# Weights split two tiles at a time, in operations twice as wide

## The chip, the cores and the metric

The kernel runs on one core of a Trainium2 chip. TensorE multiplies matrices into PSUM; VectorE, ScalarE and GpSimd work on elements; SyncE issues the transfers between HBM and SBUF. Each engine works through its own list of instructions in order and waits on semaphores for the others. The metric is device time in microseconds of one execution, as the median of several runs; one further execution was profiled.

## The reference

Two stages follow each other. The first is gated linear attention with 4 batches, 8 heads, 768 positions and head dimension 48:

```python
f = 1.0 / (1.0 + np.exp(-f_logit))
for t in range(S):
    state = f[:, :, t, :, None] * state + np.einsum('bhd,bhe->bhde', k[:, :, t], v[:, :, t])
    y[:, :, t] = np.einsum('bhd,bhde->bhe', q[:, :, t], state)
```

The second takes its output as x (4 x 768 x 384) through a gated network with a convolution of three positions along the sequence:

```python
h = np.maximum(x @ w_in, 0.0)                       # 384 -> 1024
conv_out[s] = sum_k conv_w[k] * h[s + k - 1]
out = (h * 1.0 / (1.0 + np.exp(-conv_out))) @ w_out  # 1024 -> 384
```

The three weights w_in (384 x 1024), conv_w (3 x 1024) and w_out (1024 x 384) come in as float64, all else as float32.

## The kernel before

**Recurrence.** The sequence of each batch is cut into 6 chunks of 128 positions, 24 chunks in all, numbered n. A chunk goes through these steps: the gate (exp and ln of f_logit on ScalarE, L183 and L184, loaded into fb in groups of three chunks); a running sum over positions by a product with a triangle of ones (pl, L209), from which fi and fd are made by exp (L213, L214); k times fi and q times fd (L226, L227; from the third chunk on, q on GpSimd); transposes of both (ptk, ptq, then kT, qT); the scores pa (L291), masked into am on VectorE (L293); the state (pk, L305, and stmp, st); and the values py (L328, L331), which are written as high and low part into xT (L339, L340).

**Network.** For every half sequence u, mm1 multiplies xT with w_in in eight slices f (ph, L368), ScalarE takes the relu (hb, L371), ScalarE and VectorE do the convolution (L373, L379, L380), ScalarE a tanh (L382) and VectorE the gating (L383). mm2 splits the result into gh and gl (L398, L399), multiplies them with w_out (po, L405), and ScalarE copies the output out (ob, L408). ph and po share two PSUM buffers with the tag mm.

**Weight split.** TensorE is used here with float32r operands, so each weight is wanted as a high part (what float32r holds) and a low part (the remainder). The function split_f64 makes both from the two 32-bit words of a float64: ScalarE takes the absolute value of the upper word (L101), VectorE clamps it (L102), changes the exponent's bits (L103), ScalarE clears the sign again (L104), VectorE puts the sign back (L105) and takes out the exponent (L106), and ScalarE writes the high part (L111). The low part of w_in and of the first four tiles of w_out is summed on TensorE from three products in a buffer pz (L120 to L122), from low (L118), and copied back by VectorE (w_in) or ScalarE (w_out) at L123. For the last four tiles of w_out it is made on VectorE (L113 to L115). A tile is 128 rows of a weight by 512 columns (w_in, 3 x 2 tiles) or 384 columns (w_out, 8 tiles): 14 tiles, and one small call for conv_w (24 x 128).

**Scratch.** The working pair ms (m and s side by side) lies in a buffer of the tag gl, low in one of the tag ob, the raw conv_w in one of gh. gl and gh are later the operands of mm2, ob its output; each tag has two buffers.

**What sets the order.** Every piece of work gets a number (plan, from L423 on), in units of chunks, and the pieces are emitted in the order of these numbers: the loads of w_in at -2.3 and -1.1, its splits from -0.7 and 0.9 in steps of 0.1, conv_w at 1.3, the loads of w_out at 1.3 and 1.0, its splits from 2.1 in steps of 0.35. From this the framework's scheduler, by its own modelled durations and the waits between the pieces, lays down the order of each engine's instructions before anything runs. From chunk 8 on, the recurrence's visits to TensorE (scores, state, values) are tied to one another by hand.

## Time and profile before

| | us |
|---|---|
| median of three runs | 376.55 |
| the three runs | 374.24, 376.55, 377.16 |
| the profiled execution | 371.6 |
| its span | 369.9 |

The profile's span runs from the first to the last recorded instruction; 1.7 us of the profiled execution lie around it. The granted TensorE clock was 0.987 of full speed over the span. Engines are called PE (TensorE's matmuls), PEld (its weight loads), DVE (VectorE), ACT (ScalarE), POOL (GpSimd) and SP (SyncE, which issues the transfers). A row of a group of instructions reads: line, engine, operation, written tile <- read tiles, shape, count | busy time and mean duration in ns | idle time of the engine just before them and what ended most of it. A row of one tile's instructions gives minimum, median and maximum duration in ns, and the first and the last start in us. A row of the timeline reads: start, duration, engine, line, operation, and in brackets how long the engine had been idle and for whom. A row of the waits reads: who <- for whom: us in all, times, the longest.

### The profile page before, as it was taken

What the parts mean: (1) busy time and instruction counts of PE and PEld (TensorE: products, weight loads), DVE (VectorE), ACT (ScalarE), POOL (GpSimd) and SP (SyncE); (2) the same over time, 40 slices, a digit from 0 to 9 for tenths busy, and PEclk for the clock granted to TensorE, in tenths of its full rate; (3) what the DMA queues carried; (4) which work ended last, traced back from release to release, by engine and by line L of the source; (5) the groups of instructions that cost most, each with busy time, mean ns of one, the idle gap of its engine ahead of it and who ended that gap; (6) DMA issues with size and microseconds to landing.
All of it is one profiled execution on the core that took longest, in us unless ns stands there. A gap on an engine that the chain in (4) does not pass through costs nothing.

```text
span 369.9 us, 7330 instructions
## 1 busy us (share of the span) xinstructions
PE 346.4 (94%) x2775; PEld 315.4 (85%) x2775; DVE 290.4 (79%) x455; ACT 237.9 (64%) x428; POOL 53.0 (14%) x72
## 2 busy tenths in 40 slices
PE   4799899989799998999999999999999999999993
PEld 1566678778699997999899999999999999999993
DVE  4799999999899877888689897689868875575620
ACT  3779777897977667567856566457464545665530
POOL 1111222112111410240101421041010000000000
PEclk9699999999999999999999999999999999999998
DMA  7999344315312450335113331341011002101011
GB/s 228 394 356 365 98 139 123 99 37 161 81 29 88 101 171 20 96 88 165 51 44 90 88 114 50 74 110 51 24 43 35 23 0 56 43 2 43 23 43 51
DMA packets 28853, 36.04 MB, mean 97 GB/s; under 512 B 10847, under 2 KB 20106, under 8 KB 28810
## 3 DMA queue, kind: packets, MB, share of 16 engines
q1 hardware_dynamic: 28810, 35.49, 32.1%
q8 instruction: 24, 0.39, 0.5%
q14 instruction: 19, 0.16, 0.1%
HBM read 28.37 MB, written 4.75 MB: 90 GB/s over the span
## 4 chain that ended last, share of the span: by engine, by line
PE 59%; ACT 14%; DVE 14%; DMA 6%; issue 4%; SPq 1%; ACTq 0%; DVEq 0%
PE po L405 23%; PE ph L368 20%; PE py L331 4%; DMA fb<-in_f_logit_dram 4%; PE pa L291 4%; PE py L328 3%; DMA wis<-in_moe_w_in_dram 2%; DVE g L379 2%; ACT fb L183 2%; DVE am L293 1%; PE ptk L249 1%; PE ptq L249 1%; PE pk L305 1%; ACT hb L371 1%; ACT g L373 1%
## 5 line engine op out<-in xcount | busy, mean ns | idle before, releaser
L368 PE MATMUL ph<-xT,wi 128*128 128x384 f32 x576 | 112.2, 344 | 4.5 <-ACT ob L408 2.5
L368 PEld LDWEIGHTS ph<-xT,wi 128*128 128x128 f32 x576 | 100.6, 188 | 8.2 <-ACT ob L408 3.7
L405 PE MATMUL po<-wo,gh 128*128 128x384 f32 x384 | 99.7, 340 | 0.2 <-ACT hb L371 0.2
L405 PEld LDWEIGHTS po<-wo,gh 128*128 128x128 f32 x384 | 69.6, 188 | 0.7 <-ACT hb L371 0.5
L405 PE MATMUL po<-wo,gl 128*128 128x384 f32 x192 | 66.0, 344 | 0.0
L379 DVE SCALAR_TENSOR_TENSOR g<-hb,cw,g 128x384 f32<-128x384 f32 (+1 forms) x64 | 43.5, 682 | 13.1 <-ACT g L373 12.5
L382 ACT ACTIVATE g<-g 128x768 f32<-128x768 f32 (+1 forms) x32 | 27.1, 848 | 38.7 <-DVE g L380 38.5
L371 ACT ACTIVATE hb<-ph 128x384 f32<-128x384 f32 x64 | 31.2, 489 | 23.5 <-PE ph L368 23.2
L380 DVE SCALAR_TENSOR_TENSOR g<-hb,cw,g 128x384 f32<-128x384 f32 (+1 forms) x64 | 41.8, 653 | 2.9
L399 DVE TENSOR_TENSOR gl<-g,gh 128x1024 fp32r<-128x1024 f32 (+4 forms) x34 | 32.2, 957 | 14.7 <-ACT gh L398 14.6
L383 DVE SCALAR_TENSOR_TENSOR g<-g,hb 128x768 f32<-128x768 f32 (+1 forms) x32 | 30.6, 957 | 14.1 <-ACT g L382 14.0
L227 POOL TENSOR_TENSOR qp<-qp,fd 128x384 f32<-128x384 f32 x22 | 28.9, 1313 | 87.7 <-ACT fd L214 72.1
L373 ACT ACTIVATE g<-hb,cw 128x384 f32<-128x384 f32 (+1 forms) x64 | 39.3, 619 | 2.2 <-ACT hb L371 0.4
L398 ACT CAST gh<-g 128x1024 fp32r<-128x1024 f32 (+4 forms) x34 | 26.5, 802 | 20.8 <-PE po L405 18.4
L405 PEld LDWEIGHTS po<-wo,gl 128*128 128x128 f32 x192 | 36.1, 188 | 1.1 <-issue 0.2
L293 DVE COPY_PREDICATED am<-mask,pa 128x1024 f32<-128x1024 uint8 x24 | 31.6, 1315 | 0.3
L291 PE MATMUL pa<-qT,kT 48*128 48x128 f32 x384 | 28.8, 286 | 0.4 <-ACT qT L251 0.4
L331 PE MATMUL py<-am,v 128*48 128x128 f32 x384 | 26.8, 277 | 1.6 <-DVE am L293 1.6
L226 DVE TENSOR_TENSOR kp<-kp,fi 128x384 f32<-128x384 f32 x22 | 22.7, 1033 | 6.8 <-ACT fi L213 6.6
L291 PEld LDWEIGHTS pa<-qT,kT 48*128 48x128 f32 x384 | 23.9, 187 | 3.8 <-issue 1.7
L331 PEld LDWEIGHTS py<-am,v 128*48 128x48 f32 x384 | 20.1, 122 | 6.8 <-DVE am L293 2.3
L328 PE MATMUL py<-qT,st 128*112 128x128 f32 x168 | 22.9, 275 | 0.1
(107 smaller groups left out, 432.1 us busy)
## 6 DMA issues: line engine op xcount, KB each, us to landing
kp<-in_k_dram SPq DMA_DIRECT2D x24, 256.0 KB
qp<-in_q_dram SPq DMA_DIRECT2D x24, 256.0 KB
fb<-in_f_logit_dram SPq DMA_DIRECT2D x24, 192.0 KB
v<-in_v_dram SPq DMA_DIRECT2D x24, 192.0 KB
out_dram<-ob SPq DMA_DIRECT2D x24, 192.0 KB
wis<-in_moe_w_in_dram SPq DMA_DIRECT2D x6, 512.0 KB
wos<-in_moe_w_out_dram SPq DMA_DIRECT2D x8, 384.0 KB
xT<-xT SPq DMA_DIRECT2D x48, 48.0 KB
```

The source lines that it names most:

```text
L291: nc.tensor.matmul(pa[:, j, p, :], kT[r, p, :], qT[r, p, :], start=True, stop=True)
L293: ready.setdefault(n, []).append(nc.vector.copy_predicated(am, mask, pa).ins)
L328: nc.tensor.matmul(py[:HP + D, p, :], s_b[n % 2][:, p, :], qT[:, p, :], start=(p == 0), stop=False)
L331: nc.tensor.matmul(py[HP * j:HP * j + D, p, :], vt[:, 2 * p + j, :], am[:, j, p, :], start=not inter and p == 0, stop=(p == NP - 1))
L368: nc.tensor.matmul(ph, wi[:, t, wl, f * P:(f + 1) * P], xts[b, hf][:, t, xl, :], start=(i == 0), stop=(i == 3 * KT - 1))
L371: nc.scalar.activation(hb[:, 2:HS + 2], ph, AF.Relu, scale=0.5)
L373: nc.scalar.activation(cv, hb[:, 1:n + 1], AF.Copy, scale=cw[:, 1, f:f + 1])
L379: nc.vector.scalar_tensor_tensor(cv, hb[:, 2:n + 2], cw[:, 2, f:f + 1], cv, ALU.mult, ALU.add)
L380: nc.vector.scalar_tensor_tensor(cv, hb[:, 0:n], cw[:, 0, f:f + 1], cv, ALU.mult, ALU.add)
L383: nc.vector.scalar_tensor_tensor(cv, cv, 1.0, h_b[:, fp:fp + 2, 1:n + 1], ALU.add, ALU.mult)
L399: nc.vector.tensor_tensor(lo, g[:, f:f + k], hi.bitcast(F32), ALU.subtract)
L405: nc.tensor.matmul(po, g[:, f, :], wo[:, f, wl, :], start=(i == 0), stop=(i == 3 * NF - 1))
```

## The change

split_f64 now takes several tiles at once: raw, hi and lo have a dimension k of tiles, and every operation on VectorE and ScalarE runs over all of them, 1024 or 768 elements in place of 512 or 384. Only the products on TensorE and the copy back of the low part run tile by tile; both accumulators pz of a pair are open together.

A new entry of the table CFG, kin=[[(0, 1), (1, 2)], [(0, 2), (2, 1)]], groups the three tiles of each half of w_in: tile 0 alone and tiles 1 and 2 as a pair in the first half, tiles 0 and 1 as a pair and tile 2 alone in the second. w_out goes in four pairs, emitted where the first tile of each stood. The scratch m lies in a buffer of gl, and s and low each in one of gh, all three of 1024 elements; the raw conv_w moves from gh to ob.

```diff
-    def split_f64(raw, n, hi, lo, nm, tile=0):
+    def split_f64(raw, hi, lo, nm, tile=0):
-        pr = raw.rearrange("p (n w) -> p n w", w=2)
-        lw, hw = pr[:, :, 0], pr[:, :, 1]
-        r = raw.shape[0]
-        ms = wk.tile([P, 2, WC], I32, tag="gl", name=f"ms{nm}")
-        m, s = ms[:r, 0, :n], ms[:r, 1, :n]
+        pr = raw.rearrange("p k (n w) -> p k n w", w=2)
+        lw, hw = pr[:, :, :, 0], pr[:, :, :, 1]
+        r, k, n = hw.shape
+
+        def scratch(tag, t, dt):
+            return wk.tile([P, 2 * WC], dt, tag=tag, name=f"{t}{nm}")[:r, :k * n].rearrange("p (k n) -> p k n", k=k)
+
+        m, s = scratch("gl", "m", I32), scratch("gh", "s", I32)
...
-        low = wk.tile([P, WC], F32R, tag="ob", name=f"low{nm}")[:, :n]
+        low = scratch("gh", "l", F32R)
         nc.vector.scalar_tensor_tensor(low, lw.bitcast(U32), 2.0 ** -52, sf, ALU.mult, ALU.mult)
-        pz = ps.tile([P, WC], F32, tag="mm", name=f"pz{nm}", bufs=2)[:, :n]
-        nc.tensor.matmul(pz, ident, mf, start=True, stop=False)
-        nc.tensor.matmul(pz, negr, hi, start=False, stop=False)
-        nc.tensor.matmul(pz, idr, low, start=False, stop=True)
-        (nc.vector.tensor_copy if CFG["ez"][tile] == "d" else nc.scalar.copy)(lo, pz)
+        for x in range(k):
+            pz = ps.tile([P, WC], F32, tag="mm", name=f"pz{nm}_{x}", bufs=2)[:, :n]
+            nc.tensor.matmul(pz, ident, mf[:, x], start=True, stop=False)
+            nc.tensor.matmul(pz, negr, hi[:, x], start=False, stop=False)
+            nc.tensor.matmul(pz, idr, low[:, x], start=False, stop=True)
+            (nc.vector.tensor_copy if CFG["ez"][tile + x] == "d" else nc.scalar.copy)(lo[:, x], pz)
...
-        raw = wk.tile([nk * NF, 2 * P], I32, tag="gh", name="cws")
+        raw = wk.tile([nk * NF, 2 * P], I32, tag="ob", name="cws")
...
             plan(CFG["wil"][i] + 0.01 * kt, lambda kt=kt, i=i: load_w_in(kt, i))
-            plan(CFG["wis"][i] + 0.1 * kt, lambda kt=kt, i=i: split_w_in(kt, i))
+        for kt, m in CFG["kin"][i]:
+            plan(CFG["wis"][i] + 0.1 * kt, lambda kt=kt, m=m, i=i: split_w_in(kt, m, i))
...
-        plan(CFG["wos"] + f * CFG["wo"], lambda f=f: split_w_out(f))
+        if f % 2 == 0:
+            plan(CFG["wos"] + f * CFG["wo"], lambda f=f: split_w_out(f, 2))
```

The lines of the file move by 3 to 6 (L101 becomes L104, L111 L114, L123 L127, L293 L297, L368 L372, L382 L386, L405 L409). The order of the instructions changes with the pieces. On ScalarE at the start of the program, the first two tiles of w_in stood one after the other ahead of the first chunk's fi and fd (mswi_0_188 and mswi_0_206 are the scratch of tiles 0 and 1):

```order
L101 ACTIVATE mswi_0_188<-wis_119 128x512
L101 ACTIVATE mswi_0_206<-wis_119 128x512
L104 ACTIVATE mswi_0_188<-mswi_0_188 128x512
L213 ACTIVATE fi_130<-pl_127 128x384
L214 ACTIVATE fd_129<-pl_127 128x384
L104 ACTIVATE mswi_0_206<-mswi_0_206 128x512
L111 CAST wi<-mswi_0_188 128x512
L222 COPY ft_all<-pl_127 48x4 x2
```

In the new program the same place reads (mwi_0_188 is tile 0's m, mwi_0_207 that of tiles 1 and 2):

```order
L104 ACTIVATE mwi_0_188<-wis_119 128x512
L107 ACTIVATE mwi_0_188<-mwi_0_188 128x512
L217 ACTIVATE fi_130<-pl_127 128x384
L218 ACTIVATE fd_129<-pl_127 128x384
L104 ACTIVATE mwi_0_207<-wis_119 128x1024
L114 CAST wi<-mwi_0_188 128x512
L226 COPY ft_all<-pl_127 48x4 x2
L255 COPY kT_161<-ptk_156 128x512
```

Tile 1 has left the place ahead of fi and fd and stands behind them, together with tile 2; the cast of tile 0 and the copies follow it.

On VectorE, in the middle of w_out's split, the order before was this (mswo_678, mswo_731 and mswo_783 are three of the last four tiles, g the network's first slices):

```order
L102 TENSOR_SCALAR mswo_731<-mswo_731 128x384
L113 SCALAR_TENSOR_TENSOR mswo_678<-wos_357,mswo_678 128x384
L316 TENSOR_TENSOR st_100<-stmp_1_806,ft_all 48x4x48
L103 TENSOR_SCALAR mswo_731<-mswo_731 128x384
L114 TENSOR_TENSOR mswo_678<-mswo_678,wo 128x384
L115 TENSOR_TENSOR wo<-mswo_678 128x384
L105 SCALAR_TENSOR_TENSOR mswo_731<-wos_357,mswo_731 128x384
L106 TENSOR_SCALAR mswo_731<-mswo_731 128x384
L379 SCALAR_TENSOR_TENSOR g_689<-hb,cw,g_689 128x384
```

In the new program it is this (mwo_645 and mwo_740 are the two pairs of the last four tiles):

```order
L105 TENSOR_SCALAR mwo_645<-mwo_645 128x768
L121 SCALAR_TENSOR_TENSOR lwo_566<-wos_424,swo_558 128x768
L344 TENSOR_TENSOR xT_0_302<-py_532,xT_0_302 112x4x128
L106 TENSOR_SCALAR mwo_645<-mwo_645 128x768
L297 COPY_PREDICATED am_96<-mask_86,pa_578 128x1024
L108 SCALAR_TENSOR_TENSOR mwo_645<-wos_340,mwo_645 128x768
L319 TENSOR_TENSOR stmp_0_597<-pk_588,st_100 48x192
L109 TENSOR_SCALAR swo_646<-mwo_645 128x768
L105 TENSOR_SCALAR mwo_740<-mwo_740 128x768
```

One instruction stands where two stood, and the last two pairs begin a chunk earlier, beside the fourth chunk's mask (am_96) and not beside the network's first slices.

On ScalarE around the first tanh, the order before had exp and ln of the next group (fb_1091) ahead of it:

```order
L183 ACTIVATE fb_1091<-fb_1091 128x1152
L371 ACTIVATE hb<-ph_2_753 128x384
L251 COPY kT_920<-ptk_915 128x512
L184 ACTIVATE fb_1091<-fb_1091 128x1152
L251 COPY qT_927<-ptq_922 128x512
L104 ACTIVATE mswo_783<-mswo_783 128x384
L373 ACTIVATE g_689<-hb,cw 128x384
L213 ACTIVATE fi_932<-pl_929 128x384
L214 ACTIVATE fd_931<-pl_929 128x384
L101 ACTIVATE mswo_851<-wos_357 128x384
L382 ACT_TABLE_LOAD
L382 ACTIVATE g_689<-g_689 128x2x384
```

In the new program that group is fb_1038, and it comes after two tanh and before a third (g_657 is the network's first half sequence):

```order
L386 ACTIVATE g_657<-g_657 128x2x384
L187 ACTIVATE fb_1038<-fb_1038 128x1152
L377 ACTIVATE g_657<-hb,cw 128x384
L188 ACT_TABLE_LOAD
L188 ACTIVATE fb_1038<-fb_1038 128x1152
L255 COPY kT_867<-ptk_862 128x512
L255 COPY qT_874<-ptq_869 128x512
L386 ACT_TABLE_LOAD
L386 ACTIVATE g_657<-g_657 128x2x384
```

Two loads of activation tables have come in there, one ahead of the ln and one ahead of the next tanh.

More of the change, by code (lines that the diff above doesn't have):

```diff
@@ L22 @@
 F_MIN = 2.0 ** -64
-CFG = dict(ez="ddddddaaaavvvv", ng=8, hp=4000, tb=2, groups=[3, 3, 3, 3, 3, 3, 3, 3], sg=3, f1=2.6, g1=2.6, gv=2, gl=5.2, g=3.9, l=3.2, a=1.8, b=0.8, s=0.2, v=0.5, wil=(-2.3, -1.1), wis=(-0.7, 0.9), cw=1.3, wol=(1.3, 1.0), wos=2.1, wo=0.35, m1=0.5, m1s=0.9, m2=1.5, m2s=1.2, ek=(12, 24), ec='d', er='p', tp=0, tf=2, nw=2, gd=0, q0=2, lf=3, kpool=2, eg='d', eq='p', es='d', em='d', ew='p', xb=3, nf=6, fe='a', kb=4, qb=3, vb=4, lv=2.2, cb=1, sb=3, fi=1)
+CFG = dict(ez="ddddddaaaavvvv", ng=8, kin=[[(0, 1), (1, 2)], [(0, 2), (2, 1)]], hp=4000, tb=2, groups=[3, 3, 3, 3, 3, 3, 3, 3], sg=3, f1=2.6, g1=2.6, gv=2, gl=5.2, g=3.9, l=3.2, a=1.8, b=0.8, s=0.2, v=0.5, wil=(-2.3, -1.1), wis=(-0.7, 0.9), cw=1.3, wol=(1.3, 1.0), wos=2.1, wo=0.35, m1=0.5, m1s=0.9, m2=1.5, m2s=1.2, ek=(12, 24), ec='d', er='p', tp=0, tf=2, nw=2, gd=0, q0=2, lf=3, kpool=2, eg='d', eq='p', es='d', em='d', ew='p', xb=3, nf=6, fe='a', kb=4, qb=3, vb=4, lv=2.2, cb=1, sb=3, fi=1)
 @with_exitstack
@@ L116, in split_f64, with raw_in, raw_out @@
             return
-        low = wk.tile([P, WC], F32R, tag="ob", name=f"low{nm}")[:, :n]
+        low = scratch("gh", "l", F32R)
         nc.vector.scalar_tensor_tensor(low, lw.bitcast(U32), 2.0 ** -52, sf, ALU.mult, ALU.mult)
-        pz = ps.tile([P, WC], F32, tag="mm", name=f"pz{nm}", bufs=2)[:, :n]
-        nc.tensor.matmul(pz, ident, mf, start=True, stop=False)
-        nc.tensor.matmul(pz, negr, hi, start=False, stop=False)
-        nc.tensor.matmul(pz, idr, low, start=False, stop=True)
-        (nc.vector.tensor_copy if CFG["ez"][tile] == "d" else nc.scalar.copy)(lo, pz)
+        for x in range(k):
[4 more added lines that the diff above has]
+            (nc.vector.tensor_copy if CFG["ez"][tile + x] == "d" else nc.scalar.copy)(lo[:, x], pz)
     raws = {}
-    def raw_in(kt, i):
-        if kt == 0 and ("i", i) not in raws:
+    def raw_in(i):
+        if ("i", i) not in raws:
             raws["i", i] = wk.tile([P, KT, 2 * WC], I32, tag="g32", name=f"wis{i}")
-        return raws["i", i][:, kt]
-    def raw_out(f):
-        i = f // 4
+        return raws["i", i]
+    def raw_out(i):
         if ("o", i) not in raws:
@@ L136, in raw_out, with split_w_in, split_w_out @@
                             wk.tile([P, 4, 2 * DM], I32, tag="xT", name=f"wos{i}", bufs=CFG["xb"]))
-        return raws["o", i][:, f % 4]
+        return raws["o", i]
     def load_w_in(kt, i):
-        nc.sync.dma_start(raw_in(kt, i), w_in[kt * P:(kt + 1) * P, i * WC:(i + 1) * WC].bitcast(I32))
-    def split_w_in(kt, i):
-        cs = slice(i * WC, (i + 1) * WC)
-        split_f64(raw_in(kt, i), WC, wi[:, kt, 0, cs], wi[:, kt, 1, cs], f"wi{kt}_{i}", KT * i + kt)
+        nc.sync.dma_start(raw_in(i)[:, kt], w_in[kt * P:(kt + 1) * P, i * WC:(i + 1) * WC].bitcast(I32))
+    def split_w_in(kt, k, i):
+        cs, ks = slice(i * WC, (i + 1) * WC), slice(kt, kt + k)
+        split_f64(raw_in(i)[:, ks], wi[:, ks, 0, cs], wi[:, ks, 1, cs], f"wi{kt}_{i}", KT * i + kt)
     def load_w_out(f):
-        nc.sync.dma_start(raw_out(f), w_out[f * P:(f + 1) * P, :].bitcast(I32))
-    def split_w_out(f):
-        split_f64(raw_out(f), DM, wo[:, f, 0, :], wo[:, f, 1, :], f"wo{f}", DFF // WC * KT + f)
+        nc.sync.dma_start(raw_out(f // 4)[:, f % 4], w_out[f * P:(f + 1) * P, :].bitcast(I32))
+    def split_w_out(f, k):
+        split_f64(raw_out(f // 4)[:, f % 4:f % 4 + k], wo[:, f:f + k, 0, :], wo[:, f:f + k, 1, :], f"wo{f}",
+                  DFF // WC * KT + f)
     def load_cw():
         nk = conv_w.shape[0]
-        raw = wk.tile([nk * NF, 2 * P], I32, tag="gh", name="cws")
+        raw = wk.tile([nk * NF, 2 * P], I32, tag="ob", name="cws")
         nc.sync.dma_start(raw, conv_w.bitcast(I32).rearrange("k (f x) -> (k f) x", f=NF))
         c32 = wk.tile([P, WC], F32, tag="ob", name="c32")[:nk * NF, :P]
-        split_f64(raw, P, c32, None, "cw")
+        split_f64(raw.rearrange("p (k x) -> p k x", k=1), c32.rearrange("p (k x) -> p k x", k=1), None, "cw")
         pc = ps.tile([P, nk * NF], F32, tag="mm", name="pc", bufs=2)
```

## The prediction

> **What bounds the kernel now.** I read the page's totals first, then busy time by stretch, then who waits for whom and the timeline around the places that the change touches.
>
> ```profile
> span 369.9 us, 7330 instructions
> PE 346.4 (94%) x2775; PEld 315.4 (85%) x2775; DVE 290.4 (79%) x455; ACT 237.9 (64%) x428; POOL 53.0 (14%) x72
> ```
>
> TensorE is busy in 94% of the span, so all the rest together can give back 23.5 us. Where those lie is read from the stretches (columns: length, busy time of PE, PEld, DVE, ACT and POOL with counts, granted TensorE clock, DMA share, GB/s).
>
> ```profile
> 20.00:40.00 20.00, 19.06 (x218) 13.78 (x217) 19.52 (x41) 17.91 (x42) 3.21 (x3) 1.00 0.89 319
> 40.00:60.00 20.00, 18.85 (x178) 13.95 (x177) 18.99 (x42) 15.32 (x35) 2.97 (x2) 1.00 0.50 128
> 60.00:80.00 20.00, 18.05 (x139) 14.78 (x138) 19.27 (x33) 16.80 (x32) 5.83 (x4) 1.00 0.27 76
> 80.00:103.40 23.40, 20.67 (x180) 17.54 (x179) 21.90 (x37) 21.10 (x35) 3.40 (x4) 1.00 0.39 105
> 103.40:370.00 266.60, 257.18 (x2009) 248.02 (x2006) 198.56 (x282) 156.27 (x268) 34.78 (x43) 0.99 0.23 63
> ```
>
> The weight splits run from 7.5 us to some 90 (rows below), all before the second matrix product (po, L405), which begins at about 103.4, where the last two stretches are cut. In that part the bound is VectorE: 19.5, 19.0, 19.3 of 20 us and 21.9 of 23.4, while TensorE idles 0.94 + 1.15 + 1.95 + 2.73 = 6.8 us. After 103.4 TensorE idles 9.4 us of 266.6 and sets the pace itself. So the change acts on a prefix of 103 us, and whatever lead it has when po begins goes on to the end, since the work behind that point is the same.
>
> **The change part by part.** *Fewer, wider operations.* In w_in two pairs replace four single tiles and two tiles stay single; in w_out four pairs replace eight. Each pair saves one instruction of every kind that was widened. VectorE: 5 kinds (L102, L103, L105, L106, L118) in 2 pairs of w_in and 2 of w_out, 7 kinds (L113 to L115 in L118's place) in the other 2 of w_out: 10 + 10 + 14 = 34 fewer. ScalarE: 3 kinds (L101, L104, L111) in 6 pairs: 18 fewer. The casts and matmuls of the low part stay one per tile. What one saves follows from the durations by width:
>
> ```profile
> L102 DVE TENSOR_SCALAR mswi<-mswi x6: 418/424/428, 7.5 to 28.4; 128x512 f32<-128x512 f32 x6
> L102 DVE TENSOR_SCALAR mswo<-mswo x8: 340/356/1167, 37.0 to 77.9; 128x384 f32<-128x384 f32 x8
> L105 DVE SCALAR_TENSOR_TENSOR mswi<-wis,mswi x6: 675/678/1515, 11.2 to 32.2; 128x512 int32<-128x512 int32 x6
> L105 DVE SCALAR_TENSOR_TENSOR mswo<-wos,mswo x8: 540/555/1111, 40.2 to 83.2; 128x384 int32<-128x384 int32 x8
> L383 DVE SCALAR_TENSOR_TENSOR g<-g,hb 128x768 f32<-128x768 f32 x16 | 15.3, 956 | 8.5 <-ACT g L382 8.5
> L104 ACT ACTIVATE mswi<-mswi 128x512 f32<-128x512 f32 x6 | 3.8, 632 | 0.7 <-DVE mswi L103 0.7
> L398 ACT CAST gh<-g 128x1024 fp32r<-128x1024 f32 x20 | 21.0, 1056 | 11.7 <-PE po L405 11.4
> ```
>
> Two of 384 elements take 2 x 555 = 1110 ns and one of 768 takes 956: 154 ns less. From 384 to 512 a TENSOR_SCALAR grows by 68 ns, so one of 768 is 356 + 3 x 68 = 560 against 712: 152 ns less. On ScalarE 2 x 632 - 1056 = 208 ns less. That is the saving when the next instruction waits for the result. Where it does not, neighbours overlap:
>
> ```profile
> 88.26 0.55 DVE L113 SCALAR_TENSOR_TENSOR mswo<-wos,mswo 128x384 f32<-128x384 uint32 x1
> 88.72 0.56 DVE L114 TENSOR_TENSOR mswo<-mswo,wo 128x384 f32<-128x384 f32 x1
> ...
> 91.75 0.94 DVE L383 SCALAR_TENSOR_TENSOR g<-g,hb 128x768 f32<-128x768 f32 x1
> 92.61 0.55 DVE L226 TENSOR_TENSOR kp<-kp,fi 128x384 f32<-128x384 f32 x1
> 79.75 1.14 ACT L373 ACTIVATE g<-hb,cw 128x384 f32<-128x384 f32 x2
> ```
>
> From start to start 384 elements cost 0.46 us and 768 cost 0.86: only 0.06 saved; of the two ScalarE ones in 1.14 us, each 0.62 long, 0.10 overlaps, so 0.1 is saved there. VectorE therefore gains between 34 x 0.06 = 2.0 and 34 x 0.15 = 5.1 us. In the new order about a third of the wide instructions stand directly behind the one whose result they need, so I take 23 x 0.06 + 11 x 0.15 = 3.0 us, nearer the overlapped end because the engine nearly always has the next one ready. ScalarE's 18 x 0.1 to 18 x 0.2 = 1.8 to 3.6 us I count at nothing: between 20 and 103.4 it idles 2.1 + 4.7 + 3.2 + 2.3 = 12.3 us, which hide it; without that cover they would count whole.
>
> *The first microseconds.* The timeline and the waits at the start:
>
> ```profile
> 7.93 0.43 DVE L103 TENSOR_SCALAR mswi<-mswi 128x512 int32<-128x512 int32 x1
> 9.67 0.66 ACT L101 ACTIVATE mswi<-wis 128x512 f32<-128x512 f32 x1 [2.23 <-DMA wis<-in_moe_w_in_dram]
> ...
> 11.12 0.49 ACT L214 ACTIVATE fd<-pl 128x384 f32<-128x384 f32 x1
> 11.32 1.53 SPq L140 DMA_DIRECT2D wis<-in_moe_w_in_dram  x3
> 12.01 0.62 ACT L111 CAST wi<-mswi 128x512 fp32r<-128x512 f32 x1
> ...
> PE pl L218 <- ACT fd L214: 4.5, 1, 4.5
> SPq L140 <- DMA wis<-in_moe_w_in_dram: 1.3, 1, 1.3
> ```
>
> Before, ScalarE's second L101 (tile 1 of w_in) waits for its transfer until 9.67, and L104 of tile 0, fi and fd stand behind it. Now the first tile goes alone: L103 ends at 8.4, so L104, fi and fd would end near 10.0 where fd ended at 11.6: 1.6 us earlier for TensorE, which idles 4.5 us for fd. Then the first pair waits for tiles 1 and 2. The third transfer landed near 11.3 (the next w_in load, queued for its slot on SP, was let go by it then), and with a wide L101 of 1.06 us and the cast behind it, tile 0's high part is ready at 11.3 + 1.06 + 0.62 = 13.0, where it was at 12.0 + 0.6 = 12.6. Queued behind that wait on ScalarE are the cast, the two copies into ft_all and kT. So it is between -1.6 us and, if those 0.4 and the longer chain of the pair count, +1.0. Going through the rows of VectorE and ScalarE to the second mask copy (am) with the durations above, most of the early lead is gone by then: wide instructions stand ahead of kT, qT and am. I take -0.5.
>
> *Wide instructions ahead of the recurrence.* On an engine that works in order, am (L293, for which TensorE waits) can stand behind 1.0 us where it stood behind 0.55.
>
> ```profile
> PE py L331 <- DVE am L293: 1.6, 3, 0.9
> ```
>
> Six chunks fall in this part. Between 0 and 6 x 0.35 (about half of a wide instruction's length more) = 2.1 us; I take +0.5, as only 3 of 24 visits of py waited at all. Both accumulators of a pair are open at once, in the two PSUM buffers that ph and po use too; the first ph comes behind those, and I put that at 0.
>
> *One more change of activation tables.* The split work gets done sooner, and the scheduler moves the first tanh (L382) ahead of the exp and ln of group 4. In the new order, ln and tanh alternate once more before po: two table loads more on ScalarE.
>
> ```profile
> L382 ACT ACT_TABLE_LOAD x3 | 3.8, 1283 | 0.1
> L184 ACT ACT_TABLE_LOAD x3 | 3.8, 1283 | 0.1
> ...
> 76.09 1.28 ACT L382 ACT_TABLE_LOAD   x1
> 78.66 3.44 PE L368 MATMUL ph<-xT,wi 128*128 128x384 f32 x18 [1.25 <-ACT hb L371]
> 93.88 1.28 ACT L184 ACT_TABLE_LOAD   x1
> 95.18 1.17 ACT L184 ACTIVATE fb<-fb 128x1152 f32<-128x1152 f32 x1
> 96.86 1.28 ACT L382 ACT_TABLE_LOAD   x1
> 101.07 0.44 PE L209 MATMUL pl<-cgh,tri 128*128 128x384 f32 x1 [2.23 <-ACT kT L251]
> ```
>
> 2 x 1.28 = 2.57 us on ScalarE. Both places with loads in this prefix are followed by an idle TensorE, 1.25 and 2.23 us. Between 0 and 2.57; I take their mean, +1.7. [...]
>
> **Sum.** -3.0 + 0 - 0.5 + 0.5 + 1.7 = -1.3 us. The profiled execution took 371.6 us (span 369.9 and 1.7 around it), so it would take 370.3. The median of the three runs is 376.55, 1.3% above the profiled one; on that footing 375.2.
>
> **Rivals.** *The gain comes whole (faster).* If ScalarE hides the extra loads as it idles 5.5 us between 60 and 103.4, and most wide instructions pay the dependent price: VectorE -3.8 to -4.5, ScalarE's shorter chains 0 to -1.5, the start 0 to -1.0, loads 0 to +0.5 spent where they show. That is -3.8 to -6.5, so 370.0 to 372.8. For it: VectorE's 95 to 99%. Against it: TensorE has only 6.8 + 1.6 us to give back, and each load so far reached it.
>
> *ScalarE becomes the bound (slower).* The gate of a later group must land before its exp:
>
> ```profile
> 91.71 1.17 ACT L183 ACTIVATE fb<-fb 128x1152 f32<-128x1152 f32 x1 [1.56 <-DMA fb<-in_f_logit_dram]
> ...
> SPq L241 <- DMA ft<-fd: 17.3, 17, 3.4
> ```
>
> ScalarE waited 1.56 us for group 5's transfer already, and on SP that load now stands behind the decay row's store (L233), and its last chunk behind the decay row's way back (L241), which waits 1.0 us as a rule and 3.4 at worst. Two loads and that delay make 2.57 + 1.0 to 2.57 + 3.4 = 3.6 to 6.0 us on ScalarE, of whose idle 5.5 us in 60 to 103.4 part is fixed by waits. It decides once some 3 us of it come in one piece between tanh and ln: then VectorE's 3.0 us are idle time, and the run is about 4.5 us slower: 381.
>
> [...]
>
> **Chances and range.** The forecast 0.58, the gain whole 0.24, ScalarE the bound 0.13, the port 0.05. About 1%, 3.8 us, is what a measurement of this kernel can tell from no change. So faster by over 1%: 0.24; within 1%: 0.58 + 0.05 = 0.63; slower by over 1%: 0.13. The forecast's own range, from the bounds of its terms that are likely together, is 373 to 378.5; reaching into both rivals, 370.5 to 380 leaves out about 2 in 10.
>
> **What would show it.** Right: 34 fewer instructions on VectorE and 18 fewer operations on ScalarE, the wide ones near 0.95 and 1.17 us; po starting at 100 to 103 us; VectorE still over 93% busy between 20 and 80; four table loads of tanh and four of ln in place of three each; a new TensorE gap of 1 to 2 us near the first tanh. Wrong: po starting before 99 (the gain came whole), or after 105 with ScalarE waiting for fb; TENSOR_SCALARs of 1024 elements far over 0.70 us; or a difference that arises after po has begun, which this reasoning does not have.

## The result, and the profile after

The changed kernel takes 380.67 us (median of 4 runs, 377.42 to 381.28), the kernel before beside it 376.68 (374.24 to 377.16): a ratio of 1.0125, interval 1.0082 to 1.0167. It is 1.2% slower, by more than a measurement of this kernel is uncertain, where 375.2 and no difference were forecast. The profiled execution took 380.79 us.

The totals of the page after, with two rows of its 40 slices (one digit for 9.5 us):

```profile
span 379.1 us, 7259 instructions
PE 352.5 (93%) x2775; PEld 319.4 (84%) x2775; DVE 285.9 (75%) x421; ACT 238.7 (63%) x412; POOL 53.7 (14%) x72
...
PE   5689799996999999899899999999999999999993
...
PEclk9999879998799999999999999999999999999998
```

The counts are as forecast: VectorE 455 to 421, ScalarE 428 to 412 (18 operations fewer, 2 table loads more). VectorE is busy 4.5 us less, and TensorE 6.1 us more for the same 2775 matmuls. What goes with that stands in the last row: the granted clock falls in slices 5 and 6 and again in 10 and 11, where before it fell only in slice 2 and at the end. The stretches, cut where the first second-product matmul (po) begins, at 110.9 (before: 103.4):

```profile
20.00:40.00 20.00, 18.08 (x163) 11.52 (x161) 19.33 (x34) 15.08 (x32) 2.15 (x2) 1.00 0.96 344
40.00:60.00 20.00, 17.68 (x156) 12.91 (x155) 15.92 (x27) 14.45 (x29) 2.19 (x2) 0.83 0.23 57
60.00:80.00 20.00, 20.00 (x168) 17.31 (x166) 19.78 (x29) 17.25 (x30) 6.74 (x3) 1.00 0.46 126
80.00:110.90 30.90, 25.76 (x212) 21.58 (x211) 23.59 (x35) 25.06 (x38) 5.90 (x7) 0.89 0.38 101
110.90:379.00 268.10, 258.60 (x2030) 249.12 (x2026) 197.50 (x281) 157.80 (x271) 34.18 (x43) 0.99 0.23 63
```

Behind po the two kernels take the same, 268.1 and 266.6 us. All is lost ahead of it. Two places stand out: between 40 and 60 us VectorE is busy 15.9 us of 20 (before 19.0), and from 80 on 23.6 of 30.9. VectorE, which bounded this part before, now waits there, and the mean clock is 0.83 and 0.89.

The wide instructions cost nearly what the prediction had for them: a SCALAR_TENSOR_TENSOR of 768 elements 942 ns (0.95 us forecast), a TENSOR_SCALAR of 768 554 (560), ScalarE's Abs of 1024 1140 (1.06 us). From the groups by shape:

```profile
L108 DVE SCALAR_TENSOR_TENSOR mwo<-wos,mwo 128x768 int32<-128x768 int32 x4 | 3.8, 942 | 0.0
...
L105 DVE TENSOR_SCALAR mwo<-mwo 128x768 f32<-128x768 f32 x4 | 2.2, 554 | 1.7 <-ACT mwo L104 1.7
...
L106 DVE TENSOR_SCALAR mwi<-mwi 128x1024 int32<-128x1024 int32 x2 | 1.4, 680 | 0.0
...
L104 ACT ACTIVATE mwo<-wos 128x768 f32<-128x768 f32 x4 | 3.6, 911 | 3.0 <-DVE c L112 1.3 <-DMA xT<-xT 1.2 <-ACT fd L218 0.5
...
L104 ACT ACTIVATE mwi<-wis 128x1024 f32<-128x1024 f32 x2 | 2.3, 1140 | 0.0
```

New is the idle time ahead of L104 (the Abs that opens a split), 3.0 us, 1.3 of them until VectorE's `c L112`: that is the last operation of the conv weights' small split, which frees a scratch buffer.

**The first place, 38 to 51 us.** ScalarE, and what TensorE waits for (timeline, with what ended the wait in brackets):

```profile
39.59 0.91 ACT L104 ACTIVATE mwo<-wos 128x768 f32<-128x768 f32 x1 [1.32 <-DVE c L112]
...
41.22 0.93 ACT L104 ACTIVATE mwo<-wos 128x768 f32<-128x768 f32 x1
...
42.85 0.49 ACT L217 ACTIVATE fi<-pl 128x384 f32<-128x384 f32 x1
43.22 0.50 ACT L218 ACTIVATE fd<-pl 128x384 f32<-128x384 f32 x1
```
```profile
43.78 0.52 PE L222 MATMUL pl<-ident,fd 32*48 32x1 f32 x16 [1.16 <-ACT fd L218]
...
46.23 2.02 PE L332 MATMUL py<-qT,st 128*112 128x128 f32 x8 [1.16 <-DVE xT L344]
```

Two wide Abs of w_out stand ahead of the chunk's fi and fd on ScalarE, and the first of them waits until the conv split has let go of its scratch. TensorE waits 1.16 us for fd, then 1.16 for xT.

**The second place, 84 to 99 us.** The added switch between the ln of group 4 and the tanhs: first ScalarE, then VectorE, then TensorE.

```profile
84.23 1.28 ACT L188 ACT_TABLE_LOAD   x1
85.53 1.17 ACT L188 ACTIVATE fb<-fb 128x1152 f32<-128x1152 f32 x1
...
87.67 1.28 ACT L386 ACT_TABLE_LOAD   x1
88.96 0.85 ACT L386 ACTIVATE g<-g 128x768 f32<-128x768 f32 x1
```
```profile
89.84 0.96 DVE L387 SCALAR_TENSOR_TENSOR g<-g,hb 128x768 f32<-128x768 f32 x1 [2.96 <-ACT g L386]
90.72 1.40 DVE L230 TENSOR_TENSOR kp<-kp,fi 128x384 f32<-128x384 f32 x1
```
```profile
92.22 0.98 PE L253 MATMUL ptk<-ident,kp 128*128 128x128 f32 x4 [2.73 <-issue]
...
95.68 1.95 PE L335 MATMUL py<-am,v 128*48 128x128 f32 x16 [1.63 <-DVE am L297]
```

VectorE waits 2.96 us for the tanh behind the second load, kp stands behind that on VectorE, and TensorE idles 2.73 us until kp is there (the bracket says "issue", no wait that the profile shows, but kp ends at 92.12 and the transposes that read it start at 92.22), then 1.63 more for am. Cut at the instants at which the trace's clock changes, multiples of 3.41 us apart:

```profile
41.14:44.56 3.42, 2.26 (x42) 2.00 (x42) 3.35 (x7) 3.42 (x8) 0.76 (x1) 1.00 0.43 117
44.56:47.97 3.41, 2.25 (x11) 1.84 (x9) 3.41 (x6) 3.11 (x7) 0.35 (x1) 0.50 0.05 17
47.97:51.38 3.41, 3.41 (x20) 2.53 (x19) 2.82 (x6) 1.42 (x2) 0.00 (x0) 0.50 0.00 0
...
88.92:92.34 3.42, 0.69 (x19) 0.59 (x18) 2.50 (x3) 3.38 (x8) 1.47 (x2) 1.00 0.07 11
92.34:95.75 3.41, 1.78 (x10) 1.38 (x11) 3.37 (x6) 1.90 (x4) 0.00 (x0) 0.50 0.28 64
95.75:99.17 3.42, 3.42 (x19) 2.44 (x20) 2.64 (x5) 1.42 (x2) 0.19 (x1) 0.50 0.48 84
```

Behind each of the two gaps the clock is halved for 6.83 us.

To compare runs over time I use one measure worked out from the traces: how far TensorE is behind, that is the time since the start less the work that its matmuls have done, each counted with the median step (start to next start, at most its own time) of its kind in the first trace of before. `before2` is a second profile of the kernel before, near its median; the other names are experiments, below.

```
us from start   20    40    55    75   100   120   200   300
before         8.4   7.5   8.5   9.3  10.9  10.9   7.5  -1.4
before2        9.3   8.3   9.2  10.4  10.9  15.5  12.6   3.5
after         10.6  11.5  16.5  15.5  21.9  21.7  17.9   8.8
a_noln4       10.2  11.3  16.5  15.7  19.1  19.1  14.9   5.8
wis12          9.5  10.2  10.2  10.4  16.0  16.4  11.7   2.1
cwown          7.9   9.2   8.0  10.6  14.2  13.1   9.3  -0.1
scratch5       9.9   8.7   9.4   9.8  12.2  10.9   7.9  -1.0
```

The first place costs the change 5 us (11.5 to 16.5 between 40 and 55), where before2 loses 0.9. The second costs 6.4 (15.5 to 21.9 between 75 and 100). before2 loses 4.6 of its own a little later, between 100 and 120 us, behind the two loads for group 5 (at 94.48 and 97.47 us); in the change the loads for that group come at 108.06 and 111.04 and cost nothing (21.9 to 21.7). From 55 to 120 us the two lose nearly the same, 5.2 and 6.3 us. So against before2 the second place is a loss that has moved, and of the 6.2 us between them at 120 the first place is 4.1.

A third part, 3.2 us, is there by 40 us already, 1.3 of it by 20. At 40 us every trace with the pair in the second half of w_in is 9.2 to 12.2 us behind, and those without it 7.4 to 8.9, but for one (`kCo`, 11.3, late from the start: 12.2 at 20). No run tried this part by itself.

### The profile page after: what moved, and what is told of

Its sections match the earlier page's. It is cut to its first block, busy times and chain, and to the rows that moved or that the text cites. A ratio compares the mean times of both kernels' runs of the same rounds, so it can differ in the third digit from the quotient of the medians.

```text
span 379.1 us, 7259 instructions
## 1 busy us (share of the span) xinstructions
PE 352.5 (93%) x2775; PEld 319.4 (84%) x2775; DVE 285.9 (75%) x421; ACT 238.7 (63%) x412; POOL 53.7 (14%) x72
## 4 chain that ended last, share of the span: by engine, by line
PE 69%; ACT 12%; DVE 7%; DMA 5%; issue 3%; POOL 1%; SPq 1%; ACTq 0%; DVEq 0%
PE po L409 22%; PE ph L372 21%; PE py L335 5%; PE pa L295 5%; PE py L332 4%; DMA fb<-in_f_logit_dram 3%; PE pl L213 2%; DMA wis<-in_moe_w_in_dram 2%; PE ptq L253 2%; PE ptk L253 2%; PE pk L309 2%; DVE g L383 1%; PE pzwi L124 1%; ACT fb L187 1%; POOL cgl L193 1%
## 5 line engine op out<-in xcount | busy, mean ns | idle before, releaser
L372 PE MATMUL ph<-xT,wi 128*128 128x384 f32 x576 | 114.1, 346 | 3.8 <-ACT ob L412 3.1
L372 PEld LDWEIGHTS ph<-xT,wi 128*128 128x128 f32 x576 | 100.7, 188 | 8.8 <-ACT ob L412 4.4
L409 PE MATMUL po<-wo,gh 128*128 128x384 f32 x384 | 99.6, 340 | 0.0
L409 PEld LDWEIGHTS po<-wo,gh 128*128 128x128 f32 x384 | 69.6, 188 | 0.6 <-ACT hb L375 0.3
L409 PE MATMUL po<-wo,gl 128*128 128x384 f32 x192 | 65.8, 343 | 0.0
L383 DVE SCALAR_TENSOR_TENSOR g<-hb,cw,g 128x384 f32<-128x384 f32 (+1 forms) x64 | 44.5, 699 | 14.9 <-ACT g L377 14.4
L386 ACT ACTIVATE g<-g 128x768 f32<-128x768 f32 (+1 forms) x32 | 27.1, 846 | 42.5 <-DVE g L384 42.4
L384 DVE SCALAR_TENSOR_TENSOR g<-hb,cw,g 128x384 f32<-128x384 f32 (+1 forms) x64 | 43.2, 676 | 3.0
L409 PEld LDWEIGHTS po<-wo,gl 128*128 128x128 f32 x192 | 36.1, 188 | 0.9 <-issue 0.2
L297 DVE COPY_PREDICATED am<-mask,pa 128x1024 f32<-128x1024 uint8 x24 | 31.5, 1313 | 0.2
L335 PE MATMUL py<-am,v 128*48 128x128 f32 x384 | 28.5, 289 | 1.6 <-DVE am L297 1.6
L335 PEld LDWEIGHTS py<-am,v 128*48 128x48 f32 x384 | 21.0, 128 | 7.2 <-issue 2.6
```

The source lines that it names most:

```text
L297: ready.setdefault(n, []).append(nc.vector.copy_predicated(am, mask, pa).ins)
L335: nc.tensor.matmul(py[HP * j:HP * j + D, p, :], vt[:, 2 * p + j, :], am[:, j, p, :], start=not inter and p == 0, stop=(p == NP - 1))
L372: nc.tensor.matmul(ph, wi[:, t, wl, f * P:(f + 1) * P], xts[b, hf][:, t, xl, :], start=(i == 0), stop=(i == 3 * KT - 1))
L383: nc.vector.scalar_tensor_tensor(cv, hb[:, 2:n + 2], cw[:, 2, f:f + 1], cv, ALU.mult, ALU.add)
L384: nc.vector.scalar_tensor_tensor(cv, hb[:, 0:n], cw[:, 0, f:f + 1], cv, ALU.mult, ALU.add)
L409: nc.tensor.matmul(po, g[:, f, :], wo[:, f, wl, :], start=(i == 0), stop=(i == 3 * NF - 1))
```

## The experiments

Times are medians; the ratio is to the kernel before, run beside each on the same chip (374.6 to 375.6 us). The change was timed in a set of its own, in which before took 376.68 us. So a difference to the change is given twice where it matters: by the medians, and by the ratios, which take out what differs between the sets.

**Move the switch.** At first I held the added switch (theory A) against wide w_out work ahead of the recurrence (theory B). In `g4late` the gate of group 4 is issued only behind the last tanh of the first unit; `b_g4mid` is the kernel before, with that gate put between the second and the third tanh.

```diff
+            last_tanh[0] = nc.scalar.activation(cv, cv, AF.Tanh)
...
+        with tc.issue_after(last_tanh[0].ins) if g == 4 else ExitStack():
             nc.scalar.activation(fv, fv, AF.Exp, scale=-1.0)
```

> The changed kernel, with the exp and ln of gate group 4 held back (by the scheduler's order alone) until all four tanh of the first half sequence are issued; nothing else is edited. Theory A (the extra switch of activation tables near 84 to 90 us delays fi and kp, TensorE idles 2.7 us and its granted clock then stands at 0.5 for some 6 us): 4 to 6 us faster than the changed kernel, so 375 to 377 and even with the kernel before, with the clock at 1.00 between 84 and 100 us. Theory B (wide instructions ahead of the recurrence's ones near 43 to 52 us set the loss): the dip of the clock near 46 us stays and the time stays near 380.

> The kernel before, with exp and ln of gate group 4 put between the second and the third tanh of the first half sequence, as they stand in the changed kernel. Theory A: 3 to 6 us slower than before, a TensorE gap of 2 us or more behind the two table loads, and a lower granted clock after it. Theory B: within 1 us of before.

`g4late` took 383.30 us (1.0222, 1.0182 to 1.0262), slower still. TensorE is 16.6 us behind at 100 us, where the change is 21.9 behind, but 19.6 behind at 200: the gate, late now, meets the next unit's tanhs. `b_g4mid` took 377.92 (1.007, 1.0036 to 1.0104): the switch by itself costs the kernel before 2.4 us, less than the 3 to 6 of theory A and more than the 1 of theory B, and no halved clock follows it in the trace. A miss for A as the whole cause.

**Which weight.** `win` pairs only w_in, `wout` only w_out; both have the new scratch.

```diff
-        if f % 2 == 0:
-            plan(CFG["wos"] + f * CFG["wo"], lambda f=f: split_w_out(f, 2))
+        plan(CFG["wos"] + f * CFG["wo"], lambda f=f: split_w_out(f, 1))
```
```diff
-kin=[[(0, 1), (1, 2)], [(0, 2), (2, 1)]]
+kin=[[(0, 1), (1, 1), (2, 1)], [(0, 1), (1, 1), (2, 1)]]
```

> Only w_in's pairs and the new scratch; w_out goes tile by tile. Theory A: its order also has the extra switch of tables, so 3 to 5 us slower than before. Theory B (the wide instructions of w_out's first four tiles): no dip of the clock near 46 us, within 1 us of before.

> Only w_out's pairs and the new scratch; w_in goes tile by tile. Theory A: the extra switch is there too, 3 to 5 us slower than before. Theory B: the dip near 46 us is there, and it is 3 to 4 us slower than before for that reason.

`win`: 381.75 us (1.0149, 1.0089 to 1.0209). `wout`: 372.78 (0.994, 0.9914 to 0.9966), faster than before, although its order has the added switch and its trace a halved clock near 85 us. Both theories had it 3 us or more slower. Of these two the loss comes with w_in's pairs; theory B, which put it on w_out's wide work, fell.

**Which pair, and the buffers alone.** `scratch` has both edits above, so no pair is left, only the three buffers; `kA` has w_in's pair of the first half alone, `kB` that of the second half alone; `kCo` has w_out's pairs and a pair of tiles 0 and 1 in the first half.

```diff
 kA
+kin=[[(0, 1), (1, 2)], [(0, 1), (1, 1), (2, 1)]]
 kB
+kin=[[(0, 1), (1, 1), (2, 1)], [(0, 2), (2, 1)]]
 kCo
+kin=[[(0, 2), (2, 1)], [(0, 1), (1, 1), (2, 1)]]
```

> Only the scratch buffers of the change: every tile of both weights is split alone, so no instruction is wider than before, and the order keeps before's table loads (ln only after the last tanh of the first unit). Theory P (the pair in the first half of w_in delays the second chunk): no pair, so as before, 375.5 us within 1.5. Theory T (every loss is one more ln/tanh switch with its TensorE gap and half clock): no extra switch, so as before too. If instead the scratch buffers themselves cost (rival theory B0), this one is 2 us or more above 375.5.

> The pair in the first half of w_in alone (tiles 1 and 2), everything else tile by tile; the order has no extra table switch before the second product. Theory P: the second mask copy of the recurrence at 32 to 33.5 us in place of 30 to 31, TensorE 2 to 3 us behind from there on, 377.5 to 378.5 us. Theory T: no extra switch, so 374 to 376 us.

> The pair in the second half of w_in alone (tiles 0 and 1), everything else tile by tile; here the order does have the extra ln/tanh switch in the first unit. Theory P: second mask copy at 30 to 31 us, 374 to 376 us. Theory T: a TensorE gap of 2 us or more behind the switch and 3.4 to 6.8 us of half clock, 377.5 to 380 us. Together with the run of the first half's pair this crosses the two causes.

> All pairs of w_out, and of w_in one pair in the first half, but formed of tiles 0 and 1 with tile 2 alone; second half tile by tile. No extra table switch in the order. Theory P (a pair in the first half hurts wherever it lies, since it puts wide work ahead of the second chunk): about 2.5 us above w_out's pairs alone (372.8), so 375 to 376 us. Theory T: no extra switch, so 370 to 372 us, faster than w_out's pairs alone, which carry the switch.

`scratch` 371.53 us (0.9922, 0.9893 to 0.9952): the buffers alone make the kernel faster, which no theory had. `kA` 373.66 (0.9964), `kB` 378.32 (1.0123, 1.0046 to 1.02), `kCo` 376.30 (1.0029). P (the first half's pair) falls with `kA` and `kB`, though `kCo` alone lies near its 375 to 376; T (the switch) fits `kA` (0.3 us faster than its range) and `kB`, but not `kCo`, which has no switch and missed its 370 to 372 by 4 us, and not `wout`, which has it. Something else separates them.

**The switch with the order held.** `a_noln4` and `kB_noln4` are the change and `kB` with a Relu for group 4's ln: every engine's order stays the same but for two table loads. What they compute for group 4 is not the gate.

```diff
-        nc.scalar.activation(fv, fv, AF.Ln, bias=1.0)
+        nc.scalar.activation(fv, fv, AF.Relu if g == 4 else AF.Ln, **(dict(scale=0.2) if g == 4 else dict(bias=1.0)))
```

> The changed kernel whole, but the gate of group 4 takes a Relu where it took the ln, so the ln of that group is left out; every engine's order is the same, word for word, but for two table loads less on ScalarE (the ln load near 84 us and the tanh load near 88). Theory T (the extra switch costs TensorE its gap and a halved clock behind it): 4 to 6 us less, 375 to 377 us. Theory W (the wide or joined w_in work ahead of the recurrence is what costs): only what the two loads take on ScalarE where they show, 0 to 2.6 us less, 378 to 381 us.

> The run with only the pair in the second half of w_in, with the ln of group 4 left out in the same way: the same order without the loads near 77 and 82 us. Theory T: 3.5 us or more less than that run's 378.3, 373 to 375 us, within 3 us of the run without any pair (371.5). Theory W: 376.5 to 378 us, the pair itself keeps most of its 6.8 us.

`a_noln4` 377.66 us (1.0073, 1.0039 to 1.0106) and `kB_noln4` 374.26 (0.9996, 0.9957 to 1.0036): the two loads are worth 3.0 and 4.1 us by the medians, 2.0 and 4.8 by the ratios. In `kB` that is more than the 2.57 us that they take; in the change it need not be, since the intervals of the two ratios overlap. `kB_noln4` is where theory T had it (373 to 375); `a_noln4` fell between T (375 to 377) and W (378 to 381), so the loads are less than the loss of the change. The first place remains in `a_noln4`: 16.5 us behind at 55, as in the change.

**Width or order.** `narrow` keeps pairs and buffers, and issues each widened operation once for each tile.

```diff
-        nc.vector.tensor_scalar(mf, mf, F64_LO, F64_HI, ALU.max, ALU.min)
+        for x in range(k):
+            nc.vector.tensor_scalar(mf[:, x], mf[:, x], F64_LO, F64_HI, ALU.max, ALU.min)
...
```

> The changed kernel with its pairs and its buffers, but every widened operation issued once for each tile of the pair, one tile behind the other, so that no instruction is wider than before and none waits for two transfers. The order has the extra table switch. Theory W (width and the joint wait cost): 372 to 375 us. Theory T: the switch stays, 378 to 381 us.

`narrow` took 380.52 us (1.014, 1.0078 to 1.0202), as the change: the loss needs neither the width nor one instruction's wait for two transfers. Its order is not the change's line by line, so this doesn't price the width either. `wis12` goes the other way: all pairs and widths stay, and one number of the planner moves.

```diff
-wis=(-0.7, 0.9)
+wis=(-0.7, 1.2)
```

> The changed kernel with every pair, buffer and instruction kept; only the planner's key of the second half of w_in's split is 1.2 in place of 0.9, which lets the conv weights' split and the recurrence go ahead of its last tile, and in the order that results the ln of group 4 no longer stands between the tanhs of the first unit (two table loads less before the second product). Theory O (what costs is the order that the pairs bring about, by TensorE's gaps and the halved clock behind them; pairs as such are harmless): 372 to 376 us, 5 us or more below the change. Rival W (pairs cost as such, since two tiles hold the chain and the buffers together): no more than the 3 us that the switch took, 377.5 to 380 us, with TensorE as far behind at 60 us as in the changed kernel.

375.83 us (1.0023, 0.9999 to 1.0047), 4.8 less than the change by the medians and 3.8 by the ratios: inside the range of theory O (372 to 376), though not the 5 us or more that it named. In its order the conv split comes earlier (ScalarE's part of it at 27.3 us, in the change at 33.3), one wide Abs of w_out stands ahead of fi and fd in place of two, and the ln of group 4 doesn't stand between the tanhs. It is 10.2 us behind at 40 and at 55, where the change goes from 11.5 to 16.5.

**The wait for the scratch buffer.** Looking for what the slow kernels share, I found the row of the change's waits (engine, tile and line, what it waited for; us in total, times, longest)

```profile
ACT mcw L107 <- DVE mcw L106: 2.0, 1, 2.0
...
ACT mwo L104 <- DVE c L112: 1.3, 1, 1.3
```

or one like it in `kB` (1.5 us for c), `win` and `g4late` (1.3 each), `narrow` (0.7) and, with the conv split's own L107 alone (1.1), `fill92`, which is told below: all at 378.3 us or more. `scratch`, `kA`, `wout`, `kCo` and `wis12`, all at 376.3 or less, have no wait of L104 for c. The two runs with the Relu have it too (1.3 and 1.5), and `kB_noln4` is at 374.3 all the same. So the wait alone doesn't decide.

The traces show that the first place doesn't need it either. Up to 60 us `g4late` and `fill92` have the order of the change on ScalarE, VectorE and GpSimd, instruction for instruction. In `g4late` the first Abs waits 1.31 us for c; in `fill92` it waits for nothing:

```profile
37.99 0.89 ACT L104 ACTIVATE mwo<-wos 128x768 f32<-128x768 f32 x1
...
39.60 0.91 ACT L104 ACTIVATE mwo<-wos 128x768 f32<-128x768 f32 x1
...
41.24 0.47 ACT L217 ACTIVATE fi<-pl 128x384 f32<-128x384 f32 x1
41.61 0.48 ACT L218 ACTIVATE fd<-pl 128x384 f32<-128x384 f32 x1
```

Between 40 and 55 us the two fall back by the same, 3.4 us (11.0 to 14.4) and 3.3 us (11.5 to 14.8), each with 3.41 us of halved clock; the change and `a_noln4`, in the same order with 6.83 us of it, fall back by 5.0 and 5.2. What these four share is the order, and in it the two wide Abs ahead of fi and fd. `kB` has the longest wait for c, but there fi and fd stand ahead of the Abs, and it loses 0.6 us (10.8 to 11.4). No run moves these two Abs alone. Nor is the shared buffer new: in the kernel before and in `scratch` the conv split takes a turn among gl's buffers too, and neither has the wait. `cwown` gives the conv split scratch of its own.

```diff
         def scratch(tag, t, dt):
+            if lo is None:
+                return wk.tile([P, P], dt, tag="c" + tag, name=f"{t}{nm}", bufs=1)[:r, :k * n].rearrange("p (k n) -> p k n", k=k)
```

> The changed kernel, but the small split of the conv weights has scratch of its own (128 columns, one buffer each) and no longer takes a turn in the two scratch buffers that the pairs share; pairs, widths and planner keys as changed, and the extra ln/tanh switch stays. Theory R (near 38 to 46 us ScalarE's first wide Abs of w_out waits for a buffer that the conv split still holds, fi and fd stand behind it, TensorE's gap halves its clock): that event goes, TensorE no further behind at 55 us than 12 us (16.5 in the changed kernel), 376 to 378 us. Rival (the loss there comes from the pairs wherever the conv split lies): 379 to 382 us.

> The run before with the ln of group 4 left out as well (a Relu in its place), so without the two table loads; the order is otherwise the same. If the two events near 44 and 92 us make up the loss of the change, this one is at 373 to 375 us, 6 us or more below the change and within 1% of the kernel before on its faster side. If pairs cost beside them: 376 us or more.

`cwown` 375.20 us (1.0001, 0.9968 to 1.0033), 5.5 less than the change by the medians and 4.7 by the ratios, 0.8 us below the range of theory R. Here ScalarE, and then the stretch of 20 us that showed the loss:

```profile
36.11 0.84 ACT L109 ACTIVATE mwo<-mwo 128x768 f32<-128x768 f32 x1 [0.72 <-DVE mwo L108]
36.86 0.89 ACT L106 ACTIVATE mwo<-wos 128x768 f32<-128x768 f32 x1
37.65 0.93 ACT L189 ACTIVATE fb<-fb 128x384 f32<-128x384 f32 x2
38.48 0.48 ACT L219 ACTIVATE fi<-pl 128x384 f32<-128x384 f32 x1
38.85 0.48 ACT L220 ACTIVATE fd<-pl 128x384 f32<-128x384 f32 x1
```
```profile
40.00:60.00 20.00, 19.55 (x208) 15.65 (x206) 19.69 (x32) 15.90 (x33) 2.74 (x3) 1.00 0.42 117
```

(Lines are two further down in this kernel, and behind the added matmuls in `fill92`.) The edit has changed the order: the first wide Abs of w_out stands at 30.83 us, in the change at 39.59, and only the second is left ahead of fi and fd. No Abs waits for c, and the 2.0 us that ScalarE waited for the conv split's L106 are gone as well. fd comes 4.4 us earlier than in the change (2.7 of them this execution had at 20 us already), TensorE is busy 19.55 us in place of 17.68 and VectorE 19.69 in place of 15.92, and the clock is whole in this stretch (its half lies at 74 to 81 us here). `cwown_noln4` adds the Relu: 373.71 us (0.9946, 0.9914 to 0.9978), as expected if the two places make up the loss, 7.0 less than the change by the medians and 6.7 by the ratios. So without the first place the change is level with before, and without both it is 0.5% faster. Six pairs are still no better than none (`scratch`). How the 5.5 us are shared between the waits and the order can't be told from this run alone; `fill92` speaks for the order. The sharing would then cost by the order that the scheduler makes around it.

**The clock.** `before2` is the kernel before, unchanged, for a second trace.

> The kernel before once more, unchanged, for a trace of an execution near its median, since the profiled one of 371.6 us lies below every timed run (373.35 to 377.61). Expected: 374 to 376 us, TensorE 2 to 4 us further behind than in the first trace; the part in which it falls behind tells what that trace had by luck. If it is lost before 20 us, it is the transfers and the TensorE clock of the start; if near 95 to 125 us, the table switches.

`before2` took 375.53 us. The first trace of before (371.6) and this one have the same program and nearly the same gap, in which TensorE waits 2.2 and 2.75 us for kT behind two table loads. Both cut into stretches on the grid on which their clock changed; first the earlier trace, then before2:

```profile
97.10:100.50 3.40, 1.74 (x23) 1.35 (x21) 2.34 (x5) 3.33 (x6) 0.19 (x1) 1.00 0.43 112
100.50:103.90 3.40, 2.45 (x25) 1.96 (x26) 3.12 (x6) 3.40 (x7) 0.00 (x0) 1.00 0.07 24
103.90:107.40 3.50, 3.50 (x30) 3.19 (x29) 3.40 (x6) 3.47 (x8) 1.25 (x1) 1.00 0.00 0
```
```profile
98.53:101.94 3.41, 0.66 (x9) 0.40 (x6) 2.10 (x4) 3.34 (x7) 0.19 (x1) 1.00 0.26 79
101.94:105.35 3.41, 3.22 (x23) 2.40 (x23) 3.07 (x7) 3.41 (x6) 0.00 (x0) 0.50 0.00 0
105.35:108.77 3.42, 3.42 (x11) 3.03 (x10) 3.39 (x4) 1.89 (x4) 1.24 (x1) 0.50 0.01 1
```

In the first trace the gap is spread over two stretches (1.7 and 0.9 us idle), and the clock stays. In the second it lies in one (2.75 idle), and the clock is halved for the next two. Both are 9.8 us behind at 95; at 120 the one is 10.9 behind, the other 15.5. My expectation had named the switches near 95 to 125 us as one of two answers; the clock I had not.

**Fill a gap.** `fill92` writes four more matmuls to the buffer of chunk 7's transposed k, which the transposes overwrite.

```diff
+            for _ in range(4 if nm == "k" and n == 7 else 0):
+                nc.tensor.matmul(pt.rearrange("p n t -> p (n t)"), idr, wi[:, 0, 0, :NP * P], start=True, stop=True)
```

> The changed kernel with four matmuls more (512 columns each, about 1.9 us in all, written to the buffer of chunk 7's transposed k and overwritten by it), which stand on TensorE in the 2.7 us gap ahead of those transposes near 90 us. Theory H (a stretch of 3.4 us with 1.7 us or more idle halves the granted clock for the next 3.4 to 6.8 us): the stretch at 92 to 99 us keeps the full clock in most executions, 1.5 to 3.4 us less than the change, 377 to 379 us. Rival (the gap alone costs, the clock is only a sign of it): the same 380.7 us or up to 1.9 us more.

379.33 us (1.0105, 1.007 to 1.0141): 0.3 us above the range of theory H and 1.4 below the rival's, and not by the mechanism of H. On TensorE:

```profile
88.14 1.20 PE L253 MATMUL ptk<-wi,idr 128*128 128x512 f32 x4
90.18 0.66 PE L255 MATMUL ptk<-ident,kp 128*128 128x128 f32 x4 [0.84 <-DVE kp L230]
91.04 0.66 PE L255 MATMUL ptq<-ident,qp 128*128 128x128 f32 x4 [0.20 <-POOL qp L231]
94.44 1.95 PE L337 MATMUL py<-am,v 128*48 128x128 f32 x16 [2.74 <-DVE am L299]
```

The gap ahead of the transposes is filled, and the next wait, for am, has grown from 1.63 to 2.74 us: TensorE runs ahead of VectorE here, and the clock was halved for 6.83 us all the same. That the full clock alone would give the time back isn't shown by this run.

**The version that beats both.** Only the three buffers, timed once more.

> Only the scratch buffers of the change, every tile split alone, timed again in more rounds: 371 to 372.5 us, 0.990 to 0.995 of the kernel before, if the first timing was no chance of the chip or the day; 373.5 or more if it was.

372.18 us (0.9912, 0.9878 to 0.9945). It holds: 0.9% faster than the kernel before, 2.2% faster than the change (372.18 / 380.67 = 0.978). Four of its seven timed executions had a mean granted clock of 0.995 or more; of those of before in all sets none was above 0.993. That the gain is the missing half clock near 102 us fits `before2` (15.5 us behind at 120, `scratch5` 10.9), but no run isolates it.

## Why the prediction was wrong

*Bound and place.* Right that only the part ahead of po counts: 268.1 and 266.6 us behind it. Wrong that VectorE's saved time would be lead there. VectorE did save 4.5 us of busy time, inside the 2.0 to 5.1 given for it, and spent more than that waiting. It was the bound as long as the order kept it fed; the change altered the order.

*Terms of the sum.*
- *Fewer, wider operations, -3.0.* The instructions cost what was forecast, the time gained is not seen: `kA` and `wout` are not faster than `scratch` but slower, by 2.1 and 1.3 us by the medians and 1.6 and 0.7 by the ratios (the second is within the intervals, and `wout` has the switch).
- *First microseconds, -0.5 (-1.6 to +1.0).* Not settled. fd ended at 12.8 us in the change, at 11.6 and 12.0 in the two traces of before, and at 9.6 in `kA`, which has the same pair there: `kA` and the change lie 3.2 us apart, and what the transfers and the clock have in that isn't shown.
- *Wide instructions ahead of the recurrence, +0.5 (0 to 2.1): the step that failed.* The term looked at VectorE alone, at am behind one longer instruction. TensorE's matmuls waited 1.6 us in all for am before and 1.6 after. What came instead is on ScalarE: two Abs of w_out ahead of fi and fd. The first place, where they stand, costs 5.0 us between 40 and 55 us in the change, 3.3 to 5.2 in the three other runs with the same order there, and nothing with one Abs ahead (`wis12` 0.0, `cwown` 1.2 gained). It is there with narrow instructions too (`narrow`, 3.7). That it is these two Abs, and not something else of the order, is read from the traces and not shown by a run of its own.
- *The table switch, +1.7 (0 to 2.57).* The mechanism was right, and the size about right for the change: 3.0 us there by the medians and 2.0 by the ratios, 1.5 and 2.1 in `cwown`. Only in `kB`, with 4.1 and 4.8, does it go beyond my upper end, which was the loads' own length. They sit in a chain, tanh, VectorE's gate (2.96 us idle in the change), kp, TensorE (2.73 idle), and the half clock comes behind it. On ScalarE nothing shows beside the loads' own 1.28 us each: the one at 84.23 ends at 85.51 and the ln starts at 85.53.
- *Missing terms.* I followed the PSUM buffers of the pairs, and not the scratch buffers in SBUF, in which the conv split takes its turn between pairs. Scratch of its own for it takes the two Abs apart and gives back 5.5 us by the medians, 4.7 by the ratios (`cwown`). Nor had the sum a term for what the new buffers do without any pair: 3.5 us less than before by the medians, 2.9 by the ratio (`scratch`).
- *The granted clock.* The prediction quoted it for every stretch and had no term for it. The two halved stretches of 6.83 us are up to 6.8 us of TensorE's time; `before2` has one of them.

*Footing.* The first trace of 371.6 us lay below every timed run of before (372.86 to 377.61). The prediction scaled by the median, so the ratio was not bent, but the trace lacked the half clock that `before2` has near 102 us.

*Rivals.* "ScalarE becomes the bound" (0.13) gave 381 us, close to what came. That is luck for the most part. Its chain is half right: two loads between tanh and ln did leave VectorE idle. Its trigger is wrong: ScalarE waited 0.33 us for group 4's transfer, and most of the loss is elsewhere. "The gain whole" fell; its terms as listed add up to -3.3 to -7.0, not -3.8 to -6.5, which changes nothing here. The last of the chances (0.05), qp on GpSimd held up by wide instructions on VectorE, does not show: TensorE's matmuls waited nowhere for qp in the change (before 0.2 us), its weight loads 0.2 us (before 0.4).

*What would show it.* Of the signs of being right these came: 34 and 18 fewer operations, the durations, four loads each, and a TensorE gap near the first tanhs (2.73 us, where 1 to 2 were named). These did not: po at 100 to 103 us, and VectorE over 93% busy between 20 and 80 (92%, and 80% from 40 to 60). Of the signs of being wrong, po came after 105 (110.9), but hardly with ScalarE waiting for fb.
